# A sparse-attention and mixture-of-experts kernel: the first expert job's preparation cut into attention steps, later routing tables and weight conversion moved into the expert chunks

## The chip, the cores and the metric

The kernel runs on one core of a Trainium2 chip. The metric is the device time of one execution in microseconds. The median of 3 runs of the kernel before is 794.57 us (793.63 to 795.36).

## The reference

Three layers in float32. Attention over 4 batches, 8 heads, 576 positions and 64 columns per head; heads 0 to 3 see the last 32 positions (local mask), heads 4 to 7 every 32nd position (strided mask). Its output, as 2304 rows of 512, goes to a mixture of 8 experts, where each row is sent to the one expert with the highest logit:

```python
logits = x @ w_gate + modality_bias[modality_id]
e_idx = np.argmax(logits, axis=1)
gate_w = probs[np.arange(N), e_idx]                  # softmax of the logits
for e in range(E):                                   # E = 8
    mask = e_idx == e
    h = np.maximum(x[mask] @ w1[e], 0.0)             # w1: 512 x 1024
    out[mask] = gate_w[mask, None] * (h @ w2[e])     # w2: 1024 x 512
```

A dense layer follows: `h = x @ w_in` (512 x 2048), `g = where(h > 0, h, exp(min(h, 0)) - 1)`, `g @ w_out`.

## The kernel before

Three stages share one order of instructions written out by hand: each engine runs its instructions in the order in which the Python code emits them, and waits on semaphores where data come from another engine. So an instruction that waits holds up everything emitted behind it on its engine.

**Attention** is 32 steps n (one of 4 batches, one of 4 pairs of heads, one half). Steps with n mod 8 in 0 to 3 work on strided heads (tiles of 72 x 72), the others on local heads (96 x 128). Step n emits `emit_S(n)` (scores into both banks of "S", then on VectorE masks and row maxima, 8 or 6 fused instructions at L1009, then on GpSimd the subtraction of the maxima at L1010), transposes of the next queries and keys (`emit_T`, L976), `emit_PT(n-2)`, `emit_X(n-5)` and `emit_PV(n-3)`, and `emit_exp(n-1)` on ScalarE. Scores of step n+1 need the two "S" banks back from the masks of step n. Half of the tokens (tiles 0 to 8, `NE = 9`) have their logits after step 21.

**Background.** From step 21 on, a generator `early()` prepares the first expert job, job 0: it chooses the expert of each of the first 1152 tokens, picks a frequent expert, counts places, builds a one-hot table on GpSimd (L373), multiplies it with the token numbers on TensorE (`tab_ps`, L393), gathers 512 rows by indirect DMA (L448), splits the first weights (L468, L469), scales the rows by their gates (L452) and transposes them (`trans`, L463). `bg()` is called after single VectorE instructions of `emit_X` and `emit_PV` and emits the generator's work up to its next `yield`; a `yield STEP` holds it until the next step.

**Experts.** `NS = 5` jobs of 512 rows in 8 chunks each, 40 chunks g. `stream()` emits a chunk as 8 pieces, 4 of the first product and 4 of the second one of chunk g-2. The list `plan` puts other work between the pieces by their number: the rest of attention, `choose` for the second half of the tokens (10), `place` (14), the tables (`first_tables` 16, its product 28; `more_tables(20)` 30, product 36; `more_tables(36)` 36, product 44; `dense` 53, product 64), job 1's gathers (28), scaling (38) and transposes (42, 46, 52). `conv.unit()` converts a part of the dense layer's float64 weights; it runs after chunks g = 2 to 38 with (g-2) mod 5 in 0, 1, 3.

**Dense layer.** 80 steps, each with 12 products up and 6 or 12 down. The change touches nothing of it, but 12 of the conversion units lie there, as before.

SP's queue carries nearly all loads: queries, keys and values, the expert weights (`fetch`, two DMAs of 256 KB a chunk, two to four chunks ahead), the stores of `x_dram`, the raw and converted dense weights. GpSimd's queue carries the gathers.

Of the kernel before, what the change touches and what calls it, by code (L numbers as in the profile page):

```python
# [14 lines left out]
ALU = mybir.AluOpType  # L15
# [58 lines left out]
class Background:  # L74
# [20 lines left out]
    def step(self):  # L95
        self.held = False

    def finish(self):
# [70 lines left out]
class Router:  # L169
# [104 lines left out]

    def early(self, pool, chosen):

# [21 lines left out]
        V.scalar_tensor_tensor(pr, rank[:, 0:NE], -4096.0, z, ALU.add, ALU.mult)  # L298
        yield
        V.reduce_sum(pos, pr, axis=AX.X)  # L300
# [6 lines left out]
        chosen()  # L307
        yield from self.split_places(0, NE)
        onehot = self.new_onehot(pool)
        yield from self.onehot(0, NE, onehot, self.tc.nc.gpsimd)  # L310
        finish = self.table(pool, onehot, 0, NE, 0, 4, 5, self.idx, self.gates, self.tc.nc.gpsimd)
        yield Background.STEP
        V.tensor_scalar(no, pos, 512.0, None, ALU.is_ge)
        V.tensor_scalar(self.oh[:, 0:NE, 0], pos, 512.0, None, ALU.is_lt)
        yield
        V.tensor_tensor(oh, oh, no.unsqueeze(2).to_broadcast(sh), ALU.mult)
        yield
        finish()
        yield

    def place(self, pool):
# [82 lines left out]
def ffn(tc, ctx, x_dram, part_dram, ident, router, conv, bank, w1, w2, out, run_attention):  # L404
# [151 lines left out]
    def fetch_to(g):  # L556
        while loaded[0] <= g:
            s, f = divmod(loaded[0], NCH)
            if s < NS:
                if s == len(jobs):  # L560
                    new_job(s)
                raws[loaded[0]] = fetch(jobs[s], f)
            else:
                fetch2(loaded[0] - NG)
            loaded[0] += 1
# [26 lines left out]
    def early():  # L592
        STEP = Background.STEP
        yield from router.choose(0, NE)
        yield from router.early(r_p, lambda: fetch_to(2))
        for c in range(4):
            gather(jobs[0], c)
            yield STEP if c % 2 else None
        for i in range(SPLIT):
            split_to(i)  # L600
            fetch_to(i + AHEAD - SPLIT)
            yield STEP
        for c in range(4):
            scale(jobs[0], c)
            yield STEP if c == 3 else None
        for kk in range(4):
            trans(jobs[0], kk)
            yield STEP if kk % 2 else None

# [6 lines left out]
    def close_b():  # L616
        at.close_b()
        wp = ctx.enter_context(tc.tile_pool(name="w3", bufs=1))
        add_weights(wp, NW - len(WH))
        XT.extend(x_pairs(wp, 2))  # L620
        conv.start(ctx)

    def first_tables():
        oh[0] = router.new_onehot(r_p)
        run(router.onehot(0, NT, oh[0]))
        fin.append(router.table(r_p, oh[0], 0, NT, 4, 20, 5, idx, gate))
        router.blocks(r_p)

    def more_tables(c0):
        fin.append(router.table(r_p, oh[0], 0, NT, c0, c0 + 16, 5, idx, gate))  # L630

    def dense():
        oh[0] = router.new_onehot(r_p)
        run(router.onehot(1, NT, oh[0]))
        fin.append(router.table(r_p, oh[0], 1, NT, 0, NT, 2, idxd, None))

# [4 lines left out]
    def run(gen):  # L641
        for _ in gen:
            pass

    oh, fin = {}, []
    table = lambda: fin.pop()()

    def stream():

        for g in range(NG + LAG):  # L650
# [18 lines left out]
            if g >= LAG:  # L669
# [3 lines left out]
                yield from gemm2(jobs[s], f)  # L673
            if 2 <= g < NG - 1 and (g - 2) % 5 in (0, 1, 3):
                conv.unit()
# [10 lines left out]
        (5, lambda: at.L(3, 0)), (5, lambda: at.X(31)), (8, lambda: at.L(3, 1)),  # L686
        (10, lambda: at.lg(NE, NT)), (10, lambda: run(router.choose(NE, NT))), (10, close_b),
        (14, lambda: run(router.place(r_p))), (16, first_tables),
        (28, table), (28, lambda: new_job(1)), (30, lambda: more_tables(20)), (36, table), (36, lambda: more_tables(36)), (44, table),
        (53, dense), (64, table), (66, open_y),  # L690
    ]
    plan += [(28, lambda c=c: gather(jobs[1], c)) for c in range(4)]
    plan += [(38, lambda c=c: scale(jobs[1], c)) for c in range(4)]
# [20 lines left out]


    lctx = ExitStack()
    x_loop, h_loop = bank("T", "x_ps"), bank("S", "h_ps")
# [120 lines left out]
def attention(tc, bg, q, k, v, mod, mbias, wg, x_dram, ident, router, bank):  # L838
# [148 lines left out]
    def emit_S(n):  # L987
# [16 lines left out]
        mx = m_p.tile([m, 2 * nj], F32, tag="mx", name="mx")  # L1004
        for r in range(2):
            for j in range(nj):
                mk = mask_s if pr >= 2 else (mask_0 if s == 0 and j == 0 else mask_l)
                i = nj * r + j
                nc.vector.tensor_tensor_reduce(sm[:, i], pss[r][:, j], mk, 1.0, -3.0e38, ALU.add, ALU.max, mx[:, i:i + 1])  # L1009
        nc.gpsimd.tensor_tensor(sm, sm, mx.unsqueeze(2).to_broadcast([m, 2 * nj, w]), ALU.subtract)  # L1010
        st[n] = sm
# [111 lines left out]
    for n in range(NU):  # L1123
# [29 lines left out]
        if n > 8 and n % 8 == 3:  # L1153
            load_vl(n // 8)
    emit_exp(NU - 1)
    return SimpleNamespace(PT=emit_PT, PV=emit_PV, X=emit_X, L=emit_L, lg=emit_lg, close_a=actx.close, close_b=bctx.close)
# [28 lines left out]
```

## Time and profile before

| | |
|---|---|
| median of 3 runs | 794.57 us (793.63 to 795.36) |
| the profiled execution's own time | 794.71 us |
| its span, first to last instruction | 793.0 us |
| TensorE busy (matmuls) | 763.6 us, 96% of the span |
| VectorE / ScalarE / GpSimd busy | 508.3 / 395.6 / 108.5 us |
| mean granted TensorE clock | 0.991 |

The span and the profiled execution's own time differ by 1.7 us, which lie outside of the first and last instruction. TensorE is idle for 793.0 - 763.6 = 29.4 us. A granted clock of 1.00 is 2.4 GHz, one of 0.5 is 1.2 GHz; a value between them in a short stretch says that both levels occurred in it.

### The profile page before, as it was taken

What the parts mean: (1) busy time and instruction counts of PE and PEld (TensorE: products, weight loads), DVE (VectorE), ACT (ScalarE), POOL (GpSimd) and SP (SyncE); (2) the same over time, 40 slices, a digit from 0 to 9 for tenths busy, and PEclk for the clock granted to TensorE, in tenths of its full rate; (3) what the DMA queues carried; (4) which work ended last, traced back from release to release, by engine and by line L of the source; (5) the groups of instructions that cost most, each with busy time, mean ns of one, the idle gap of its engine ahead of it and who ended that gap; (6) DMA issues with size and microseconds to landing.
All of it is one profiled execution on the core that took longest, in us unless ns stands there. A gap on an engine that the chain in (4) does not pass through costs nothing.

```text
span 793.0 us, 12672 instructions
## 1 busy us (share of the span) xinstructions
PE 763.6 (96%) x4513; PEld 636.5 (80%) x4513; DVE 508.3 (64%) x1321; ACT 395.6 (50%) x759; POOL 108.5 (14%) x140
## 2 busy tenths in 40 slices
PE   6999988989999999999899999999999999999995
PEld 5989876868888888888788788888888888888885
DVE  3768779798867677576477565565666454544443
ACT  3667646433544454445376555554565444444442
POOL 4533372022001020000000101001001010101011
PEclk9999999999999999999999999999999999999999
DMA  9587695545566575454232221033133030201111
GB/s 159 120 186 172 151 241 102 153 148 186 179 204 222 172 227 183 163 184 136 93 122 80 94 79 54 27 107 119 41 95 131 1 107 0 84 24 41 66 41 67
DMA packets 100302, 94.37 MB, mean 119 GB/s; under 512 B 45433, under 2 KB 78731, under 8 KB 100235
## 3 DMA queue, kind: packets, MB, share of 16 engines
q1 hardware_dynamic: 95056, 78.79, 34.8%
q0 software_dynamic: 4480, 14.68, 5.4%
q8 instruction: 37, 0.61, 0.3%
q14 instruction: 30, 0.25, 0.1%
q10 hardware_dynamic: 699, 0.04, 0.1%
HBM read 70.95 MB, written 22.54 MB: 118 GB/s over the span
## 4 chain that ended last, share of the span: by engine, by line
PE 50%; POOLq 0%; POOL 0%; DVE 0%; issue 0%
PE o_ps L797 8%; PE o_ps L799 8%; PE o_ps L798 8%; PE h_ps L711 8%; PE h_ps L710 8%; PE h_ps L712 8%; POOLq L1181 0%; POOL out_dram L813 0%; DVE part L812 0%
## 5 line engine op out<-in xcount | busy, mean ns | idle before, releaser
L773 DVE SCALAR_TENSOR_TENSOR t<-e,t 128x512 f32<-128x512 f32 (+1 forms) x80 | 51.1, 638 | 110.7 <-ACT e L771 110.7
L710 PE MATMUL h_ps<-xh,wh 128*128 128x512 f32 (+1 forms) x320 | 119.1, 372 | 2.2 <-PEq L723 2.2
L712 PE MATMUL h_ps<-xh,wl 128*128 128x512 f32 (+1 forms) x320 | 119.3, 373 | 0.0
L711 PE MATMUL h_ps<-xl,wh 128*128 128x512 f32 (+1 forms) x320 | 119.2, 372 | 0.0
L797 PE MATMUL o_ps<-wh,gh 128*128 128x512 f32 x288 | 113.3, 393 | 0.0
L798 PE MATMUL o_ps<-wl,gh 128*128 128x512 f32 x288 | 112.9, 392 | 0.0
L799 PE MATMUL o_ps<-wh,gl 128*128 128x512 f32 x288 | 112.9, 392 | 0.0
L770 ACT ACTIVATE t<-h_ps 128x512 f32<-128x512 f32 (+1 forms) x80 | 44.2, 552 | 99.8 <-PE h_ps L712 92.3
L775 ACT CAST gh<-r 128x512 fp32r<-128x512 f32 (+1 forms) x80 | 46.2, 578 | 81.5 <-DVE r L774 81.5
L776 DVE TENSOR_TENSOR gl<-r,gh 128x512 fp32r<-128x512 f32 (+1 forms) x80 | 51.1, 639 | 51.5 <-ACT gh L775 51.5
L469 DVE TENSOR_TENSOR wl<-wraw,wh 128x1024 fp32r<-128x1024 f32 x56 | 69.2, 1235 | 12.8 <-ACT wh L468 11.0
L710 PEld LDWEIGHTS h_ps<-xh,wh 128*128 128x128 f32 x320 | 60.6, 189 | 14.3 <-issue 2.6
L711 PEld LDWEIGHTS h_ps<-xl,wh 128*128 128x128 f32 x320 | 60.6, 189 | 11.9
L712 PEld LDWEIGHTS h_ps<-xh,wl 128*128 128x128 f32 x320 | 60.5, 189 | 11.0
L504 PE MATMUL y_ps<-hh,wh 128*128 128x512 f32 x160 | 64.6, 404 | 0.0
L797 PEld LDWEIGHTS o_ps<-wh,gh 128*128 128x128 f32 x288 | 54.1, 188 | 12.5 <-DVE o L808 0.7
L799 PEld LDWEIGHTS o_ps<-wh,gl 128*128 128x128 f32 x288 | 54.1, 188 | 12.1
L485 PE MATMUL h_ps<-xh,wh 128*128 128x512 f32 x160 | 63.7, 398 | 0.0
L506 PE MATMUL y_ps<-hh,wl 128*128 128x512 f32 x160 | 63.3, 395 | 0.0
L505 PE MATMUL y_ps<-hl,wh 128*128 128x512 f32 x160 | 63.2, 395 | 0.0
L798 PEld LDWEIGHTS o_ps<-wl,gh 128*128 128x128 f32 x288 | 54.1, 188 | 11.1
L487 PE MATMUL h_ps<-xh,wl 128*128 128x512 f32 x160 | 62.9, 393 | 0.0
(180 smaller groups left out, 1393.4 us busy)
## 6 DMA issues: line engine op xcount, KB each, us to landing
wraw<-in_moe_w_dram SPq DMA_DIRECT2D x80, 256.0 KB
raw<-in_moe_w_in_dram SPq DMA_DIRECT2D x16, 512.0 KB
raw<-in_moe_w_out_dram SPq DMA_DIRECT2D x16, 512.0 KB
w_f<-cv_r SPq DMA_DIRECT2D x32, 256.0 KB
wraw<-w_f SPq DMA_DIRECT2D x16, 512.0 KB
part_dram<-o POOLq DMA_DIRECT2D x18, 256.0 KB, 3.0
part<-part_dram SPq DMA_DIRECT2D x18, 256.0 KB
qn<-in_q_dram SPq DMA_DIRECT2D x8, 288.0 KB
```

What stands on the lines that cost most here:

```text
L469: nc.vector.tensor_tensor(WL[i], raw, WH[i].bitcast(F32), ALU.subtract)
L485: nc.tensor.matmul(ps, lhsT=a, rhs=job.xh[kk], start=kk == 0, stop=False)
L487: nc.tensor.matmul(ps, lhsT=b, rhs=job.xh[kk], start=False, stop=kk == 3)
L504: nc.tensor.matmul(ps, lhsT=a, rhs=hh, start=f == 0, stop=False)
L505: nc.tensor.matmul(ps, lhsT=a, rhs=hl, start=False, stop=False)
L506: nc.tensor.matmul(ps, lhsT=b, rhs=hh, start=False, stop=f == NCH - 1)
L710: nc.tensor.matmul(ps[:, 0:n], lhsT=a, rhs=yh, start=kk == 0, stop=False)
L711: nc.tensor.matmul(ps[:, 0:n], lhsT=a, rhs=yl, start=False, stop=False)
L712: nc.tensor.matmul(ps[:, 0:n], lhsT=b, rhs=yh, start=False, stop=kk == 3)
L797: nc.tensor.matmul(ps, lhsT=a, rhs=WH[i][:, 512:1024], start=first, stop=False)
L798: nc.tensor.matmul(ps, lhsT=a, rhs=WL[i][:, 512:1024], start=False, stop=False)
L799: nc.tensor.matmul(ps, lhsT=b, rhs=WH[i][:, 512:1024], start=False, stop=last)
```

## The change

Four parts. (1) `bg.flush()` at the end of each attention step emits all background work up to the next `STEP`, in place of one piece after each VectorE instruction; the `STEP` marks are set anew, the weights are fetched chunk by chunk (`fetch_to(0)`, `(1)`, `(2)`, `(3)`) instead of three chunks at once, and job 0's rows are scaled on GpSimd instead of VectorE. The three instructions that take job 0's rows out of the counts become `others()` and move behind the second `choose` at piece 10. (2) In strided steps the 8 fused mask-and-maximum instructions become two additions over 288 columns and one maximum over 576. (3) The tables that no early job needs move: `more_tables(20)` from piece 30 to 84, `more_tables(36)` from 36 to 104, the dense table from 53 to seven parts at 120 to 144, their products to 100, 116 and 164. Their buffers come from a new pool. (4) Conversion units run from chunk 6 on, 7 in 10 chunks (24 units) in place of 3 in 5 from chunk 2 on (23 units).

```diff
--- before.py
+++ after.py
@@ -94,6 +94,11 @@
 
     def step(self):
         self.held = False
+
+    def flush(self):
+
+        while self.gens and not self.held:
+            self()
 
     def finish(self):
         while self.gens:
@@ -272,7 +277,7 @@
         V.tensor_copy(self.lof[:, q, 0:n], self.lo[:, q, 0:n])
         yield
 
-    def early(self, pool, chosen):
+    def early(self, pool, chosen, more):
 
         V = self.tc.nc.vector
         t = lambda shape, dt, name: pool.tile(shape, dt, name=name)
@@ -296,7 +301,7 @@
         yield
 
         V.scalar_tensor_tensor(pr, rank[:, 0:NE], -4096.0, z, ALU.add, ALU.mult)
-        yield
+        yield Background.STEP
         V.reduce_sum(pos, pr, axis=AX.X)
         V.tensor_tensor(key[0:1], key[0:1], self.rev[0:1], ALU.mult)
         yield
@@ -306,17 +311,23 @@
         V.tensor_scalar(self.star, kmax[0:1], -1.0, float(E), ALU.mult, ALU.add)
         chosen()
         yield from self.split_places(0, NE)
+        yield Background.STEP
         onehot = self.new_onehot(pool)
-        yield from self.onehot(0, NE, onehot, self.tc.nc.gpsimd)
+        for i, _ in enumerate(self.onehot(0, NE, onehot, self.tc.nc.gpsimd)):
+            yield Background.STEP if i == 1 else None
         finish = self.table(pool, onehot, 0, NE, 0, 4, 5, self.idx, self.gates, self.tc.nc.gpsimd)
+        more()
         yield Background.STEP
-        V.tensor_scalar(no, pos, 512.0, None, ALU.is_ge)
-        V.tensor_scalar(self.oh[:, 0:NE, 0], pos, 512.0, None, ALU.is_lt)
-        yield
-        V.tensor_tensor(oh, oh, no.unsqueeze(2).to_broadcast(sh), ALU.mult)
-        yield
         finish()
         yield
+
+        def others():
+
+            V.tensor_scalar(no, pos, 512.0, None, ALU.is_ge)
+            V.tensor_scalar(self.oh[:, 0:NE, 0], pos, 512.0, None, ALU.is_lt)
+            V.tensor_tensor(oh, oh, no.unsqueeze(2).to_broadcast(sh), ALU.mult)
+
+        self.others = others
 
     def place(self, pool):
 
@@ -592,20 +603,23 @@
     def early():
         STEP = Background.STEP
         yield from router.choose(0, NE)
-        yield from router.early(r_p, lambda: fetch_to(2))
+        yield STEP
+        yield from router.early(r_p, lambda: fetch_to(0), lambda: fetch_to(1))
         for c in range(4):
             gather(jobs[0], c)
-            yield STEP if c % 2 else None
-        for i in range(SPLIT):
-            split_to(i)
-            fetch_to(i + AHEAD - SPLIT)
-            yield STEP
+            yield STEP if c == 1 else None
+        split_to(0)
+        fetch_to(2)
+        yield STEP
+        split_to(1)
+        fetch_to(3)
+        yield
         for c in range(4):
-            scale(jobs[0], c)
-            yield STEP if c == 3 else None
+            scale(jobs[0], c, nc.gpsimd)
+            yield STEP if c == 1 else None
         for kk in range(4):
             trans(jobs[0], kk)
-            yield STEP if kk % 2 else None
+            yield STEP if kk % 2 == 0 else None
 
     bg.early = early
     at = run_attention(bg)
@@ -619,20 +633,24 @@
         add_weights(wp, NW - len(WH))
         XT.extend(x_pairs(wp, 2))
         conv.start(ctx)
+        late.append(tctx.enter_context(tc.tile_pool(name="late", bufs=1)))
 
     def first_tables():
-        oh[0] = router.new_onehot(r_p)
+        oh[0] = router.new_onehot(late[0])
         run(router.onehot(0, NT, oh[0]))
-        fin.append(router.table(r_p, oh[0], 0, NT, 4, 20, 5, idx, gate))
+        fin.append(router.table(late[0], oh[0], 0, NT, 4, 20, 5, idx, gate))
         router.blocks(r_p)
 
     def more_tables(c0):
-        fin.append(router.table(r_p, oh[0], 0, NT, c0, c0 + 16, 5, idx, gate))
-
-    def dense():
-        oh[0] = router.new_onehot(r_p)
-        run(router.onehot(1, NT, oh[0]))
-        fin.append(router.table(r_p, oh[0], 1, NT, 0, NT, 2, idxd, None))
+        fin.append(router.table(late[0], oh[0], 0, NT, c0, c0 + 16, 5, idx, gate))
+
+    def dense(i):
+        if i == 0:
+            oh[0] = router.new_onehot(late[0])
+            oh[1] = router.onehot(1, NT, oh[0])
+        next(oh[1], None)
+        if i == NT // 3:
+            fin.append(router.table(late[0], oh[0], 1, NT, 0, NT, 2, idxd, None))
 
     def open_y():
         rctx.close()
@@ -642,7 +660,8 @@
         for _ in gen:
             pass
 
-    oh, fin = {}, []
+    oh, fin, late = {}, [], []
+    tctx = ExitStack()
     table = lambda: fin.pop()()
 
     def stream():
@@ -671,7 +690,7 @@
                 if f == NCH - 1 and s:
                     jobs[s].start = start_of(router.tab[0:1, s, 1:2])
                 yield from gemm2(jobs[s], f)
-            if 2 <= g < NG - 1 and (g - 2) % 5 in (0, 1, 3):
+            if 6 <= g < NG - 1 and (g - 6) % 10 not in (3, 6, 9):
                 conv.unit()
             if g == NG - 1:
 
@@ -684,11 +703,12 @@
         (3, lambda: at.PV(30)), (3, lambda: at.X(29)), (3, lambda: at.PT(31)),
         (4, lambda: at.PV(31)), (4, lambda: at.X(30)),
         (5, lambda: at.L(3, 0)), (5, lambda: at.X(31)), (8, lambda: at.L(3, 1)),
-        (10, lambda: at.lg(NE, NT)), (10, lambda: run(router.choose(NE, NT))), (10, close_b),
+        (10, lambda: at.lg(NE, NT)), (10, lambda: run(router.choose(NE, NT))), (10, lambda: router.others()), (10, close_b),
         (14, lambda: run(router.place(r_p))), (16, first_tables),
-        (28, table), (28, lambda: new_job(1)), (30, lambda: more_tables(20)), (36, table), (36, lambda: more_tables(36)), (44, table),
-        (53, dense), (64, table), (66, open_y),
+        (28, table), (28, lambda: new_job(1)), (66, open_y),
+        (84, lambda: more_tables(20)), (100, table), (104, lambda: more_tables(36)), (116, table), (164, table),
     ]
+    plan += [(120 + 4 * i, lambda i=i: dense(i)) for i in range(NT // 3 + 1)]
     plan += [(28, lambda c=c: gather(jobs[1], c)) for c in range(4)]
     plan += [(38, lambda c=c: scale(jobs[1], c)) for c in range(4)]
     plan += [(n, lambda kk=kk: trans(jobs[1], kk)) for kk, n in enumerate((42, 46, 52, 52))]
@@ -713,6 +733,7 @@
 
 
 
+    tctx.close()
     lctx = ExitStack()
     x_loop, h_loop = bank("T", "x_ps"), bank("S", "h_ps")
     ahead = [bank("ST"[j], "h2_ps") for j in range(2)]
@@ -1003,10 +1024,15 @@
         sm = s_p.tile([m, 2 * nj, w], F32, tag="sm", name="sm")
         mx = m_p.tile([m, 2 * nj], F32, tag="mx", name="mx")
         for r in range(2):
+            if pr >= 2:
+                nc.vector.tensor_tensor(sm[:, nj * r:nj * r + nj], pss[r], mask_s.unsqueeze(1).to_broadcast([m, nj, w]), ALU.add)
+                continue
             for j in range(nj):
-                mk = mask_s if pr >= 2 else (mask_0 if s == 0 and j == 0 else mask_l)
+                mk = mask_0 if s == 0 and j == 0 else mask_l
                 i = nj * r + j
                 nc.vector.tensor_tensor_reduce(sm[:, i], pss[r][:, j], mk, 1.0, -3.0e38, ALU.add, ALU.max, mx[:, i:i + 1])
+        if pr >= 2:
+            nc.vector.reduce_max(mx, sm, axis=AX.X)
         nc.gpsimd.tensor_tensor(sm, sm, mx.unsqueeze(2).to_broadcast([m, 2 * nj, w]), ALU.subtract)
         st[n] = sm
 
@@ -1152,6 +1178,7 @@
             load_vs(n // 8 + 1)
         if n > 8 and n % 8 == 3:
             load_vl(n // 8)
+        bg.flush()
     emit_exp(NU - 1)
     return SimpleNamespace(PT=emit_PT, PV=emit_PV, X=emit_X, L=emit_L, lg=emit_lg, close_a=actx.close, close_b=bctx.close)
 
```

## Rows read from the trace of the kernel before

**Rows 1.** Waits of TensorE: in total us, times, longest us
```profile
PE ps_tr L976 <- DMA qn<-in_q_dram: 3.0, 3, 1.3
PE tab_ps L393 <- DVE A L388: 2.9, 1, 2.9
```
**Rows 2.** Stretches: us, busy us of each engine, clock, DMA share, GB/s
```profile
110.00:115.00 5.00, 4.33 (x41) 4.04 (x39) 4.04 (x28) 2.46 (x6) 4.31 (x4) 0.68 1.05 277
...
175.00:180.00 5.00, 5.00 (x23) 4.09 (x21) 4.35 (x9) 0.00 (x0) 2.01 (x3) 0.69 0.93 330
...
123.41:127.78 4.37, 3.31 (x40) 2.70 (x38) 4.14 (x14) 3.39 (x6) 1.45 (x1) 1.00 0.54 112
127.78:133.42 5.64, 4.89 (x42) 3.73 (x42) 5.61 (x25) 2.78 (x6) 1.47 (x1) 1.00 0.01 3
133.42:136.00 2.58, 1.00 (x8) 0.82 (x9) 2.51 (x10) 0.98 (x2) 1.47 (x1) 1.00 0.57 145
```
**Rows 3.** Timeline of TensorE: start, us, instruction, idle before
```profile
108.42 0.37 PE L393 MATMUL tab_ps<-A,onehot 128*128 128x20 bf16 x9 [1.91 <-POOL A L388]
...
115.65 0.44 PE L976 MATMUL ps_tr<-ident,qn 96*128 96x96 f32 x3 [1.32 <-DMA qn<-in_q_dram]
...
174.35 1.16 PE L393 MATMUL tab_ps<-A,onehot 128*128 128x80 bf16 x18 [2.90 <-DVE A L388]
...
180.81 0.72 PE L463 MATMUL x_ps<-ident,xg 128*128 128x128 f32 x4
```
**Rows 4.** Timeline of GpSimd
```profile
2.58 1.83 POOL L914 MEMSET vs<- 64x2080 f32 x1
...
99.54 1.15 POOL L1010 TENSOR_TENSOR sm<-sm,mx 72x576 f32<-72x576 f32 x1 [2.62 <-ACT sm L1014]
101.55 5.26 POOL L373 TENSOR_SCALAR onehot<-iota,pos_lof 128x128 bf16<-128x128 bf16 x9 [0.86 <-DVE rs L1061]
...
107.87 0.50 POOL L388 TENSOR_TENSOR A<-oa,vals 128x180 bf16<-128x180 bf16 x1
108.32 1.16 POOL L1010 TENSOR_TENSOR sm<-sm,mx 72x576 f32<-72x576 f32 x1
...
123.40 1.47 POOL L1010 TENSOR_TENSOR sm<-sm,mx 96x768 f32<-96x768 f32 x1 [5.64 <-DVE mx L1009]
...
171.52 1.57 POOL L448 DMA_INDIRECT xg<-x_dram,idx  x1 [14.89 <-DMA wraw<-in_moe_w_dram]
...
176.67 0.95 POOL L448 DMA_INDIRECT xg<-x_dram,idx  x1 [0.30 <-issue]
```
**Rows 5.** Timeline of VectorE
```profile
99.90 0.82 DVE L303 TENSOR_SCALAR pos<-pos 128x9 f32<-128x9 f32 x1
...
106.87 2.71 DVE L316 TENSOR_TENSOR oh<-oh,no 128x72 bf16<-128x72 bf16 x1
...
168.69 0.41 DVE L143 TENSOR_SCALAR cv_t<-raw 128x512 int32<-128x512 int32 x1
169.13 0.69 DVE L144 SCALAR_TENSOR_TENSOR cv_t<-raw,cv_t 128x512 int32<-128x512 int32 x1
...
170.60 0.17 DVE L396 SCALAR_TENSOR_TENSOR idx<-tab_sb 128x16 int32<-128x16 f32 x1
...
179.42 0.87 DVE L452 TENSOR_SCALAR xg<-xg,gates 128x512 f32<-128x512 f32 x2
```
**Rows 6.** Groups of instructions, 0 to 260 us, by shape: busy us, mean ns, idle
```profile
L1009 DVE CUSTOM_DVE_ANT_0 sm<-ps_sc,mask_s 72x72 f32<-72x72 f32 x128 | 20.6, 223 | 9.2 <-PE ps_sc L1001 9.2
...
L1066 DVE TENSOR_TENSOR xs<-ps_v,rs 72x256 f32<-72x256 f32 x32 | 12.1, 415 | 0.5
...
L340 DVE TENSOR_REDUCE pos<-places 128x36 f32<-128x324 f32 x1 | 0.5, 491 | 0.0
```
**Rows 7.** Queue of SP, timeline: the query loads of the last pair
```profile
109.12 1.42 SPq L875 DMA_DIRECT2D qn<-in_q_dram  x2
```
**Rows 8.** Tile xg (gathered rows), 100 to 260 us: issue to landing
```profile
DMA to landing us min/median/max: 4.0/5.2/7.6
```

## The prediction, made before the changed kernel ran

> **What bounds the kernel now.** I read the totals first: TensorE is busy for 96% of the span, so a change can gain only where TensorE is idle or slow. The list of its waits, then its timeline, say where. After 181 us it waits only at the check that leads to the dense layer, which isn't touched; all that this change can win lies in two places, steps 21 to 31 of attention and the first six expert chunks. There the reader is to see four things. TensorE waits 1.91 us for the table that GpSimd multiplies, 1.32 us for the queries of the last pair and 2.90 us for a table that VectorE multiplies [rows 1, 3]. After the 1.91 and after the 2.90 the granted clock of a 5 us stretch is 0.68 and 0.69, which is the 2.4 GHz level with the 1.2 GHz level in it, at 5 x 0.32 = 1.6 us of work lost; after the 1.32 it isn't [rows 2]. In steps 30 and 31 and up to the first expert product VectorE is busy 4.14 + 5.61 + 2.51 of 12.59 us and TensorE only 3.31 + 4.89 + 1.00 = 9.20 [rows 2], so VectorE sets the pace there and 3.4 us could be won. And in the experts the stall of 2.90 us has slack behind it: job 1's first transposes start at 180.81, just behind the scaling that began at 179.42 [rows 3, 5].
>
> **Steps 21 to 27.** `flush` puts each group of background work as a lump between the `emit_PV` of a step and the masks of the next one on VectorE. Until now pieces stood between other instructions and filled their latencies. VectorE is nearly always busy here, so what counts is what now stands ahead of the masks of step 24. New ahead of them are the nine small instructions that end in the places (L300 to L272), at about 0.13 us each, since one takes 0.17 us alone and the next starts earlier [rows 5]: 1.2 us (bounds: nothing if they fill gaps, 2.0 if one waits as L303 did for 0.82). So GpSimd's subtraction of step 24 starts not at 99.54 but at 100.74. Behind it GpSimd has 1.15 for it, nine one-hot rows of 5.26 in all, the subtraction of step 25 at 1.15 and the product A at 0.45 [rows 4]. The sum is 108.75. Splitting the nine into 6 and 3 changes their order, not their sum, and TensorE's table product still stands at the end of step 26, so it starts 0.4 later than at 108.42 [rows 3]. The stall stays and the slow stretch of 1.6 us behind it too. The masks in the new form cost VectorE more: 8 fused at 20.6/128 = 0.16 are 1.3 us a step; two additions at 0.41 (0.378 for 256 columns, times 288/256) and one maximum of 576 columns, between 0.49 (324 columns) and 0.87 (in proportion), say 0.75, are 1.6 [rows 6]. That is 0.3 a step, 4.5 us in 16 steps. I cost it at nothing on the path, since TensorE waits for the banks, which now come back after 0.8 instead of 1.3; if that cover is gone, steps 24 to 27 cost 1.2 more.
>
> **Step 28.** The last queries are issued at 109.12 behind three chunks of weights, 1.5 MB [rows 7]. Now one chunk stands ahead of them on SP's queue, and the second follows them. They come some 3 us earlier and the wait of 1.32 goes [rows 3]; step 29 starts 0.4 - 1.3 = 0.9 earlier. What is moved behind, values and two chunks, is needed from step 31 and from chunk 1 on.
>
> **Steps 29 to 31.** Here is the price. The rows are now scaled on GpSimd, two at the end of step 28 and two at the end of step 29, and the first transposes stand right behind them in TensorE's order, ahead of the scores of step 30. TensorE must wait for: the masks of step 29, GpSimd's subtraction behind them (at 123.40 before [rows 4]), and two scalings. GpSimd's price for a scaling of 128x512 isn't in the trace. The nearest rows are a fill at 1.83/2080 a column, 0.45 for 512, and a comparison of 128 columns at 5.26/9 = 0.58, 2.3 in proportion [rows 4]; I take 1.0, near the fill, since a fixed part is in the 0.58. Also, the second weight split on VectorE stands beside the first two scalings. The row shows what such neighbours do: L316, 72 columns, took 2.71 us, to 109.58, while GpSimd ran A and the subtraction to 109.48 [rows 4, 5]. I take 0.7 us for that (bounds 0 and 2.3). So the subtraction starts at 123.40 - 0.9 + 0.7 = 123.2, ends at 124.7, and the transposes start at 126.7. TensorE comes there at 123.41 - 0.9 = 122.5, where step 30 began before [rows 2], and idles for 4 us. From there its own work is the 9.20 of rows 2, to 135.9, and the clock falls, as after 1.91 and 2.90: 137.5, against 136.0. Attention ends 1.5 us later. With the bounds it is between 2 earlier (0.45, no neighbours, no slow stretch) and 6 later.
>
> The Trainium skill, page "SBUF — State Buffer", section "Who interferes with whom", names as those that contend with GpSimd the VectorE instructions in a two-port mode or with both inputs in SBUF, and says that the loser waits for the whole instruction. The trace agrees for L316. By that rule the weight split waits for both scalings, 1.3 us more than I took, and the sum would be 1.3 higher.
>
> **Experts up to chunk 6.** `others()` adds three VectorE instructions behind `choose`, and TensorE's `place` needs their result: 0.8 us (0.5 by three at 0.17, 3.2 if GpSimd is in the way as for L316 [rows 5]). It delays TensorE and VectorE alike. The conversion of chunk 3 no longer stands ahead of the first table's read-out: 0.41 + 0.69 = 1.1 less [rows 5]. So the row numbers of job 1, at 170.60 before, come at 170.3. The four gathers take from 171.52 to 176.67 to issue [rows 4]; without the neighbouring tables perhaps 4.0, so the last goes at 175.2. From issue to landing it takes 4.0 at least, 5.2 in the median [rows 8]; before it was about 4.0, since the last of the four scalings began by 180.7. I take 4.5, and 0.5 for the scaling: 180.2. TensorE, without the stall of 2.90 and the 1.6, is there at 180.81 - 2.90 - 1.6 + 0.8 = 177.1 and waits for 3 us. So the transposes start 0.6 earlier than at 180.81, but the slow stretch, which before lay in the shadow of this chain, now comes after it: -0.6 + 1.6 = +1.0 (bounds: -1.1 without it, +2.1 at the median landing). The tables and the conversions that come later lie under expert products, in a stretch where TensorE waits for nothing, and cost nothing; if that cover fails, one table costs what it did, 2.9.
>
> **The rivals.** A: the sum, 1.5 + 1.0 = 2.5 later. B: the waits only change their names, and no slow stretch is added: -0.1 and -0.6, so 794.0. For it speaks that 1.32 and 1.6 us of waiting left the clock alone; against it that the two waits I expect are 3 and 4. C, faster: scaling on GpSimd is done when TensorE gets there, because a scaling takes 0.45 to 0.7 and the split doesn't wait. Its place is the end of step 29; it decides if the transposes start before 124.3, a wait of under 1.9. Then attention ends at 133.4, 2.6 earlier, and with B's or A's experts it is 791.5 to 793.1. For it speaks VectorE's load in steps 30 and 31, which it lifts. D: GpSimd takes 2.3 a scaling: the transposes start at 131, and it ends near 801. E, that the change does not do what it says: the tables leave chunk 5 and nothing is won, since the gather sets that time anyway; it is part of A and B.
>
> The page "GPSIMD Engine Reference", section 4.1, of the Trainium skill holds that instructions with one input run on GpSimd at roughly line rate. The row of the fill bears it out, that of the comparison doesn't. By it a scaling would be about 0.65, an estimate from that page, and case C has its chance from there.
>
> **How the numbers follow.** The sum is made against the profiled execution: 794.7 + 2.5 = 797.2. It lies 0.14 above the median of the runs, so the forecast is 797.1. What a measurement here can tell from no change is about 0.2%, 1.6 us: below 793.0 is faster, above 796.2 slower. Chances: A 0.45 (795.0 to 799.5), B 0.22 (793 to 796), C 0.25 (789 to 793.3), D 0.08. Slower: most of A and all of D, 0.46; same: the rest of A and most of B, 0.27; faster: C and the edge of B, 0.27. The range of 8 in 10 takes in C and A and leaves out D: 790.0 to 800.0.
>
> **What would show it.** In the profile after: the wait of the small table on GpSimd near 108.8; no wait for queries in step 28; a wait of job 0's first transposes for scaled rows on GpSimd, near 4 us, with a slow stretch behind it; no wait for A at chunk 5, but one of about 3 us of job 1's transposes for gathered rows. The prediction is wrong if scaling on GpSimd takes under 0.7 us or over 2, if steps 23 to 26 lose more than 1 us to late masks, or if the gathers land sooner than 4 us after their issue.

## The result, and the profile after

The changed kernel takes 802.01 us in the median of 9 runs (797.06 to 805.55), the kernel before 795.06 us (793.63 to 798.60) beside it on the same chip: a ratio of 1.0082, with a 95% interval of 1.0058 to 1.0105. It is slower, by 7 us where the forecast said 2.5, and 802.0 lies outside the range that was given. The profiled execution spans 800.3 us, 7.3 more than before.

The waits of TensorE after, longest in total first (us in total, times, longest):

```profile
PE x_ps L474 <- DVE xg L463: 7.8, 4, 5.0
PE ps_tr L997 <- POOL vs L936: 4.6, 1, 4.6
PE x_ps L474 <- POOL xg L463: 3.9, 2, 2.7
PE tab_ps L404 <- POOL A L399: 2.6, 1, 2.6
PE h_ps L730 <- PEq L744: 1.8, 1, 1.8
PE x_ps L474 <- DVE tab_sb L406: 1.0, 1, 1.0
PE ps_tr L997 <- DMA qn<-in_q_dram: 0.8, 1, 0.8
```

Against [rows 1] the wait for the table of VectorE is gone, and the one query wait that is left (0.76 us, at 49.88) lies far ahead of step 21. New are the two kinds of `x_ps`: 3.9 us for job 0's rows, scaled on GpSimd, and 7.8 us for job 1's rows. The timeline of TensorE shows where they stand:

```profile
106.80 0.37 PE L404 MATMUL tab_ps<-A,onehot 128*128 128x20 bf16 x9 [2.58 <-POOL A L399]
...
123.55 0.33 PE L474 MATMUL x_ps<-ident,xg 128*128 128x128 f32 x1 [2.69 <-POOL xg L463]
125.09 0.48 PE L474 MATMUL x_ps<-ident,xg 128*128 128x128 f32 x1 [1.21 <-POOL xg L463]
...
175.93 0.30 PE L474 MATMUL x_ps<-ident,xg 128*128 128x128 f32 x1 [0.53 <-DVE xg L463]
176.79 0.33 PE L474 MATMUL x_ps<-ident,xg 128*128 128x128 f32 x1 [0.56 <-DVE xg L463]
182.11 0.47 PE L474 MATMUL x_ps<-ident,xg 128*128 128x128 f32 x1 [4.99 <-DVE xg L463]
184.31 0.47 PE L474 MATMUL x_ps<-ident,xg 128*128 128x128 f32 x1 [1.73 <-DVE xg L463]
```

Stretches behind these waits (busy us of TensorE's products, of its weight loads, of VectorE, ScalarE and GpSimd, then the granted clock, DMA share and GB/s; compare [rows 2]):

```profile
105.00:110.00 5.00, 3.20 (x42) 3.10 (x42) 3.08 (x9) 1.61 (x5) 4.38 (x7) 0.80 1.10 250
110.00:115.00 5.00, 5.00 (x55) 4.53 (x54) 3.62 (x16) 3.51 (x9) 4.53 (x4) 0.86 1.13 302
125.00:130.00 5.00, 4.91 (x36) 4.41 (x37) 2.56 (x14) 2.62 (x5) 1.28 (x2) 0.50 0.01 2
180.00:185.00 5.00, 1.16 (x3) 0.79 (x4) 0.97 (x2) 0.18 (x1) 0.00 (x0) 0.50 0.18 62
185.00:190.00 5.00, 5.00 (x14) 3.81 (x13) 2.44 (x3) 1.94 (x3) 0.00 (x0) 0.51 0.00 0
```

In the last one TensorE is busy throughout and gets 0.51, the 1.2 GHz level: after the wait of 7.8 us it works from 184.31 to about 189.9 at half clock, 2.8 us of work lost.

Where the time went, by the start of the same instruction on TensorE in both traces:

| up to | before | after | later in this part by |
|---|---|---|---|
| scores of step 4 | 23.21 | 21.31 | -1.90 |
| scores of step 27 | 108.72 | 107.10 | +0.28 |
| scores of step 29 | 119.10 | 116.13 | -1.35 |
| first expert product | 136.01 | 135.11 | +2.07 |
| product of the first large table | 164.98 | 164.81 | +0.73 |
| last transposes of job 1 | 189.51 | 194.43 | +5.09 |
| first product of the dense layer | 389.33 | 396.50 | +2.25 |

Of the first line 0.42 us come from the masks: from the scores of step 1 to those of step 2 it is 2.82 us in each of the five profiles with the old form and 2.40 in the twelve with the new one, since TensorE gets the banks back sooner there. The rest is the landing of the first loads, which the change doesn't touch; step 4 starts anywhere from 21.05 to 22.64 in the profiles with the new masks and from 21.45 to 23.21 in those with the old ones, so the early start belongs to these two executions and not to the change. What counts is the sixth line, and the other engines tell why. VectorE in front of job 1's transposes, GpSimd's gathers and SP's queue, after:

```profile
172.88 1.22 DVE L480 TENSOR_TENSOR wl<-wraw,wh 128x1024 fp32r<-128x1024 f32 x1 [0.24 <-ACT wh L479]
175.30 0.48 DVE L463 TENSOR_SCALAR xg<-xg,gates 128x512 f32<-128x512 f32 x1 [1.19 <-DMA xg<-x_dram,idx]
176.25 0.49 DVE L463 TENSOR_SCALAR xg<-xg,gates 128x512 f32<-128x512 f32 x1 [0.47 <-DMA xg<-x_dram,idx]
181.57 0.49 DVE L463 TENSOR_SCALAR xg<-xg,gates 128x512 f32<-128x512 f32 x1 [4.83 <-DMA xg<-x_dram,idx]
183.77 0.49 DVE L463 TENSOR_SCALAR xg<-xg,gates 128x512 f32<-128x512 f32 x1 [1.72 <-DMA xg<-x_dram,idx]
...
170.26 1.62 POOL L459 DMA_INDIRECT xg<-x_dram,idx  x1 [14.17 <-DVE gates L410]
...
175.23 0.95 POOL L459 DMA_INDIRECT xg<-x_dram,idx  x1 [0.30 <-issue]
...
171.00 0.38 SPq L486 DMA_DIRECT2D wraw<-in_moe_w_dram  x1
...
174.13 0.38 SPq L486 DMA_DIRECT2D wraw<-in_moe_w_dram  x1
174.71 0.35 SPq L488 DMA_DIRECT2D wraw<-in_moe_w_dram  x1
175.11 0.43 SPq L131 DMA_DIRECT2D raw<-in_moe_w_in_dram  x1
```

VectorE itself waits for the rows: the last gather is issued at 175.23 and its scaling starts at 183.77, 8.5 us later. Between 174.13 and 175.11 SP issued 1 MB, the weights of chunk 10 and the first conversion load. In the kernel before, the weights of chunk 10 were issued at 179.52, behind all gathers, because their buffer came free only when VectorE had split chunk 7 (the load starts 0.03 us behind the split's end, before and after). VectorE and SP of the kernel before:

```profile
176.70 1.66 DVE L388 TENSOR_TENSOR A<-oa,vals 128x1440 bf16<-128x1440 bf16 x1
178.28 1.21 DVE L469 TENSOR_TENSOR wl<-wraw,wh 128x1024 fp32r<-128x1024 f32 x1
...
179.52 0.38 SPq L475 DMA_DIRECT2D wraw<-in_moe_w_dram  x1
```

The split stood behind the tables that the change moved away. After, the same split begins at 172.88, 5.4 us sooner.

### The profile page after: what moved, and what is told of

It reads as the page before. It is cut to its first block, busy times and chain, and to the rows that moved or that the text cites. A ratio compares the mean times of both kernels' runs of the same rounds, so it can differ in the third digit from the quotient of the medians.

```text
span 800.3 us, 12473 instructions
## 1 busy us (share of the span) xinstructions
PE 766.7 (96%) x4513; PEld 638.1 (80%) x4513; DVE 507.7 (63%) x1109; ACT 395.8 (49%) x759; POOL 116.1 (15%) x144
## 5 line engine op out<-in xcount | busy, mean ns | idle before, releaser
L497 PE MATMUL h_ps<-xl,wh 128*128 128x512 f32 x160 | 63.2, 395 | 0.0
```

Of the source, the lines that this page charges most:

```text
L497: nc.tensor.matmul(ps, lhsT=a, rhs=job.xl[kk], start=False, stop=False)
```

## The experiments

Times are medians; each ratio is against runs of the kernel before on the same chip, with its 95% interval. Not all runs were made on one chip, so where two runs are compared with each other their ratios count; 0.0010 is 0.8 us. Four runs undo or hold back something in the changed kernel and one repeats it, four do one part in the kernel before and one adds the held loads to such a part, five look for a better version.

**VectorE scales job 0's rows again.**

```diff
-            scale(jobs[0], c, nc.gpsimd)
+            scale(jobs[0], c)
```

> The changed kernel, with the four rows of job 0 scaled on VectorE as before. Theory (GpSimd's 1.6 us a scaling stands in TensorE's order): the waits of job 0's first transposes, 2.7 + 1.2 us, go, and with them about half of the slow stretch behind them, while VectorE gets 4 x 0.49 us more; attention ends some 3 us earlier and the whole comes to 799 us. Rival (VectorE sets the pace in steps 29 to 31, whoever scales): the 2 us on VectorE and a later second weight split take it back, 802 us, no difference.

Measured: 797.94 us, ratio 1.0022 (1.0003 to 1.0042), 4 to 5 us better than the changed kernel, where the theory had 3. But not all of it is job 0's: a wait of 2.05 us stays there, now for VectorE's scaling, since the transposes still stand right behind it; and in this profile the last row block of job 1 came 6.7 us after its issue (174.59 to 181.28), not 8.5.

**The tables back at their old places, the rest of the change kept.**

```diff
-        (84, lambda: more_tables(20)), (100, table), (104, lambda: more_tables(36)), (116, table), (164, table),
+        (30, lambda: more_tables(20)), (36, table), (36, lambda: more_tables(36)), (44, table), (64, table),
     ]
-    plan += [(120 + 4 * i, lambda i=i: dense(i)) for i in range(NT // 3 + 1)]
+    plan += [(53, lambda i=i: dense(i)) for i in range(NT // 3 + 1)]
```

> The changed kernel, with the two later routing tables and the dense one back at their old places in chunks 4 to 8. Theory (the tables' work on VectorE held the weight split of chunk 7, this held the load of chunk 10, and so the gathered rows of job 1 came in 4.3 us): the wait for a table at chunk 5 is back, 2.9 us, but the rows land in 4 to 5 us again instead of 8.5, and the transposes of job 1 follow the scaling; 802 - 5 = 797 us. Rival (the gathers are late for another reason): 2.9 us and the slow stretch come on top, 803 to 806 us.

Measured: 794.99 us, ratio 0.9978 (0.9956 to 1.0000). The whole loss of 7 us hangs on the tables' places. A wait for a table is back (1.8 us), the weights of chunk 10 are issued at 179.82, and the last row, issued at 177.31, is scaled at 181.96, 4.7 us later.

**The two loads held until job 1's rows are scaled.** A small transfer on SP's queue reads the scaled rows, so SP issues what follows only then. It writes one column of a scratch buffer that is written over later. The changed kernel with this one line more:

```diff
+    plan += [(38, lambda: nc.sync.dma_start(part_dram[NT - 1, :, 0:1], jobs[1].xg[3][:, 0:1]))]
```

> The changed kernel with one small transfer more on SP's queue: it reads one column of the last scaled row block of job 1, so that the weights of chunk 10 and the first conversion load are issued only when job 1's rows have been gathered and scaled. Theory (these two loads, 1 MB, delay the gathers): the last gather lands 4 to 5 us after its issue, the transposes wait some 4 us instead of 7.8 and the slow stretch is shorter; 802 - 5 = 797 us. Rival (the gathers take 6 to 8 us whatever stands beside them): the wait stays 7 to 8 us and the time 802; held loads come late for chunk 10 and it may be slower still.

Measured: 797.09 us, ratio 1.0024 (1.0004 to 1.0044). VectorE, GpSimd and SP of this kernel:

```profile
179.41 0.49 DVE L463 TENSOR_SCALAR xg<-xg,gates 128x512 f32<-128x512 f32 x1 [0.74 <-DMA xg<-x_dram,idx]
180.71 0.49 DVE L463 TENSOR_SCALAR xg<-xg,gates 128x512 f32<-128x512 f32 x1 [0.81 <-DMA xg<-x_dram,idx]
...
175.03 1.49 POOL L459 DMA_INDIRECT xg<-x_dram,idx  x1 [0.30 <-issue]
176.82 0.94 POOL L459 DMA_INDIRECT xg<-x_dram,idx  x1 [0.30 <-issue]
...
181.22 0.33 SPq L714 DMA_DIRECT2D part_dram<-xg  x1
181.82 0.39 SPq L486 DMA_DIRECT2D wraw<-in_moe_w_dram  x1
```

The last row comes 3.9 us after its issue, not 8.5, and the transposes wait 3.3 us, not 7.8. By the ratios 4.6 us come back. The theory stands, and the rival falls.

**The conversion from chunk 8 on, so that of the two loads only the weights stand beside the gathers.**

```diff
-            if 6 <= g < NG - 1 and (g - 6) % 10 not in (3, 6, 9):
+            if 8 <= g < NG - 1 and (g - 8) % 10 not in (4, 9):
```

> The changed kernel with the conversion units from chunk 8 on instead of 6, in a slightly denser pattern, so that their first load comes behind the gathers of job 1 and only the weights of chunk 10 stand beside them. If the conversion's load is what delays the rows, they land in 4 to 5 us and the time is 797 us, as with both loads held; if the weights are, 802 us as in the changed kernel; if each does its half, 799 to 800 us.

Measured: 798.90 us, ratio 1.0037 (1.0013 to 1.0062). The last row, issued at 176.81, is scaled at 182.24, 5.4 us later. So each load takes its part: with neither of them 3.9, with the weights alone 5.4, with both 6.7 to 8.5 us. The conversion's load alone was not run; its part is the difference.

**The changed kernel a second time.**

> The changed kernel once more, for a second profile. If the landing of job 1's rows is the same each time, the last gather lands 8 to 9 us after its issue again and the wait ahead of job 1's transposes is 7 to 8 us; if it scatters with the order of the packets, the two differ by 1 us or more (in the kernel with VectorE's scaling, which is the same in the experts, the last one took 6.7 us). The slow stretch after the wait of step 26 lasts 1.7 us of lost work, as in the first profile, or 4 to 5, as in two of the others.

Measured: 802.82 us. The last row, issued at 176.29, is scaled at 184.78: 8.5 us again, and the transposes wait 7.8 us again; against the 6.7 of the kernel with VectorE's scaling, which is the same in the experts, the landing scatters by some 2 us. So does the slow stretch behind the wait of step 26. First this profile, then that of the kernel with VectorE's scaling, whose instructions are the same up to there; the wait ahead is 2.59 us in both:

```profile
105.00:110.00 5.00, 2.65 (x35) 2.49 (x35) 3.31 (x12) 1.12 (x3) 4.63 (x7) 0.79 0.99 245
110.00:115.00 5.00, 5.00 (x41) 4.60 (x40) 2.71 (x8) 3.06 (x6) 4.05 (x4) 0.53 1.08 292
115.00:120.00 5.00, 5.00 (x64) 4.41 (x63) 3.88 (x20) 3.87 (x10) 3.00 (x2) 1.00 1.21 219
```

```profile
105.00:110.00 5.00, 2.79 (x42) 2.53 (x42) 3.34 (x11) 1.76 (x5) 4.49 (x6) 0.90 0.92 235
110.00:115.00 5.00, 5.00 (x41) 4.61 (x40) 3.38 (x13) 2.63 (x5) 4.42 (x4) 0.50 1.07 290
115.00:120.00 5.00, 5.00 (x38) 4.27 (x38) 1.64 (x13) 3.23 (x7) 1.91 (x2) 0.58 1.21 210
```

With the first profile (0.80 from 105 to 110 and 0.86 from 110 to 115, 1.7 us lost) that makes 1.7, 3.4 and 5.1 us of work lost for the same wait. Each of the three comes twice in the six profiles whose instructions are the same up to there: 1.7 also with the tables at their old places, 3.4 with the conversion from chunk 8, 5.1 with the held loads.

**Single parts in the kernel before**: the masks, the conversion from chunk 6, job 0's new preparation (with `flush` and `others`), and the tables' new places, each alone and as in the diff of the change.

> The kernel before with the mask edit alone (two additions and one maximum instead of eight fused instructions in the steps of the strided pairs). Theory (VectorE has the 0.3 us a step to spare, and step 4 starting 1.9 us earlier in the changed kernel's trace is an early load, not the masks, which do not come before step 4): 795 us, no difference. Rivals: TensorE gets the score banks back sooner and the 1.9 us are real, 793; or VectorE's 0.3 us a step lie on the path in steps 21 to 31, 796 to 797.

Measured: 794.56 us, ratio 0.9991 (0.9969 to 1.0013): no difference that the runs show; the 0.42 us of step 2 lie within the interval. (That the masks do not come before step 4 was an error: steps 0 to 3 are strided ones.)

> The kernel before with the conversion units from chunk 6 on alone. Theory (its work lies under expert products): 795 to 796 us, no difference. Rival (by itself it frees VectorE ahead of the stall for a table at chunk 5 and the 1.1 us are seen): 793 to 794.5 us.

Measured: 794.72 us, ratio 1.0002 (0.9983 to 1.0020): no difference.

> The kernel before with the new preparation of job 0 alone (the lumps, one chunk of weights ahead of the queries, scaling on GpSimd, the three instructions put off until behind the attention); masks, tables and conversion stay. Theory (two waits of 2.7 and 1.2 us for GpSimd's scaling against the query wait and VectorE's load in steps 30 and 31, which go): within 1 us of before, 795 us. Rival, the term of the forecast (attention ends 1.5 us later): 796.5 us.

Measured: 796.23 us, ratio 1.0011 (0.9990 to 1.0033). The interval holds both answers. The waits for GpSimd's scaling are there, 2.7 and 1.2 us.

> The kernel before with the later routing tables and the dense one moved as in the changed kernel, and nothing else. Theory (without the tables the weight split of chunk 7 ends early, the load of chunk 10 starts some 5 us sooner, and the gathers land late behind it): the wait of 2.9 us at chunk 5 is replaced by one of 4 to 8 us before the transposes of job 1, with a slow stretch behind it: 798 to 801 us. Rival (the tables' move is harmless by itself, the loss comes from the two preparations together): 793 to 795 us.

Measured: 801.54 us, ratio 1.0070 (1.0046 to 1.0095). This part alone makes the kernel slower by nearly as much as all four. The wait at chunk 5 is gone; its place in the list is taken by this:

```profile
PE x_ps L463 <- DVE xg L452: 6.1, 4, 3.3
```

**The tables' new places and the held loads, in the kernel before**, with the same small transfer.

> The kernel before with the tables moved (801.5 us alone) and the loads of chunk 10 and of the conversion at chunk 5 held until job 1's rows are scaled, by the same small transfer. Theory (those loads delay the gathers): rows land 3.5 to 4.5 us after their issue, 801.5 - 4 = 797 to 798 us. Rival (the rows are as late as that by the time of their issue alone): 800 to 802 us.

Measured: 797.58 us, ratio 1.0035 (1.0014 to 1.0056), 4.0 us less than with the tables alone by the medians, 2.8 by the ratios. The last row comes in 3.7 us (173.81 to 177.52) where it took 5.75 (173.85 to 179.60).

**A version to beat both.** On top of the held loads (`MID` is a new mark that holds the background work until before the next `emit_X`; its few lines are left out here):

```diff
...
-            scale(jobs[0], c, nc.gpsimd)
-            yield STEP if c == 1 else None
+            scale(jobs[0], c)
+            yield STEP if c == 1 else Background.MID if c == 3 else None
...
-        (84, lambda: more_tables(20)), (100, table), (104, lambda: more_tables(36)), (116, table), (164, table),
+        (84, lambda: more_tables(20)), (96, table), (96, lambda: more_tables(36)), (112, table), (164, table),
...
-    plan += [(n, lambda kk=kk: trans(jobs[1], kk)) for kk, n in enumerate((42, 46, 52, 52))]
+    plan += [(n, lambda kk=kk: trans(jobs[1], kk)) for kk, n in enumerate((48, 50, 52, 54))]
...
```

> A version to beat both: the changed kernel with the scaling of job 0 on VectorE and its first transposes in the middle of step 30, the loads of chunk 10 and of the conversion held until job 1's rows are scaled, job 1's transposes 2 to 6 pieces later in the stream (at 48, 50, 52 and 54), and the two later tables' products away from the transposes of job 2. Theory (each wait was met because TensorE came too early to rows that were on their way): no wait over 1 us between step 28 and chunk 8, 802 - 4 - 5 - 2 = 790 to 792 us. Rival (the work that stands at those places is only pushed and something else, such as the weights of chunk 10, comes late): 795 us and over.

Measured: 786.74 us, ratio 0.9882 (0.9854 to 0.9911): 1.2% faster than the kernel before and better than expected. TensorE's longest waits, and two of its stretches:

```profile
PE ps_tr L1003 <- DMA qn<-in_q_dram: 6.1, 4, 4.8
PE tab_ps L409 <- POOL A L404: 2.5, 1, 2.5
PE h_ps L736 <- PEq L750: 1.9, 1, 1.9
PE ps_tr L1003 <- DMA kn<-in_k_dram: 0.8, 1, 0.8
PE x_ps L479 <- DVE xl L473: 0.7, 1, 0.7
```

```profile
125.00:130.00 5.00, 4.33 (x54) 3.79 (x53) 4.93 (x24) 3.42 (x7) 1.47 (x1) 1.00 0.08 22
180.00:185.00 5.00, 5.00 (x26) 4.07 (x25) 4.09 (x6) 2.94 (x5) 3.08 (x3) 1.00 0.92 314
```

No wait for rows is left, of either job, and the clock stays at 1.00 where it was 0.50.

> The first combination (786.7 us) without the held loads. Theory (the loads delay the rows by some 3 to 4 us, of which the 4 us that the transposes were put off hide most): the first transposes of job 1 wait 1 to 4 us again, 788 to 791 us. Rival (putting the transposes off was all that was needed): 787 us.

Measured: 790.13 us, ratio 0.9932 (0.9911 to 0.9952). The transposes wait 2.6 us again; the last row, issued at 172.92, is scaled at 179.83, 6.9 us later. The theory's numbers; the hold is worth 3.4 us by the medians, 4.0 by the ratios, even where the transposes come later.

**The wait for the small table.** Three tries moved its product (and the gathers behind it) from the end of step 26.

```diff
...
         more()
-        yield Background.STEP
+        yield Background.MID
         finish()
-        yield
...
             gather(jobs[0], c)
-            yield STEP if c == 1 else None
+            yield
```

> The version before it, and the product of the first small table in the middle of step 27 instead of at the end of step 26, with the four gathers right behind it. Theory: the wait of 2.6 us for GpSimd goes and the slow stretch behind it with it, 2 to 5 us less than the version before it, 786 to 789 us. Rival (the rows of job 0 come later by as much and the transposes of step 30 or GpSimd's subtraction of step 28 wait for it): no difference to the version before it.

Measured: 792.21 us, ratio 0.9955 (0.9934 to 0.9976), 5.5 us worse than the first combination. It doesn't answer the question that it was made for: the product ended up ahead of `emit_PV` of step 26, 1.2 us earlier, not later. The wait grew from 2.5 to 3.8 us, and 110 to 120 us ran at 0.50; but 2.6 us were followed by about 10 us at half clock in two other profiles, so this run doesn't show that the longer wait made the stretch longer.

Then the product where it was meant to be (against the run above):

```diff
...
         more()
+        yield Background.STEP
         yield Background.MID
         finish()
```

> The first combination (786.7 us), with the product of the small table really later: at the X of step 27, some 2 us of TensorE's work behind its present place (the second combination had put it in the middle of step 26, 1.2 us earlier instead of later, and its wait was 3.8 instead of 2.5 us and TensorE at half clock for 10 us). Theory: the wait is under 0.5 us, no slow stretch follows, 786.7 - 2.5 - 1.7 = 782 to 784 us. Rival (GpSimd's four gathers then stand ahead of its subtraction of step 28, and something after it waits): 786 us or more.

Measured: 791.41 us, ratio 0.9940 (0.9919 to 0.9961). The wait is gone (0.28 us), but what it had covered now stands in the open: the weights of chunk 1, for which ScalarE waits 3.5 us with queries behind them, so that TensorE waits 3.0 us for ScalarE; and the gathered rows, for which VectorE waits 2.8 and 1.4 us with the masks behind them, so that TensorE waits 2.5 us for masks there.

And with the second split and the scaling a step later:

```diff
...
         fetch_to(2)
         yield STEP
+        yield STEP
         split_to(1)
```

> The combination with the table's product at the X of step 27, and the second weight split and the scaling of job 0 one step later than there, so that they do not wait for loads that are still on their way. Theory (in that version TensorE was 4 us earlier in step 28 than the weights of chunk 1 and the gathered rows): no wait of more than 1 us in steps 27 to 29, 783 to 786 us. Rival (the rows and VectorE's splits are then late for the first expert product): 787 us or more, no better than the first combination.

Measured: 786.31 us, ratio 0.9873 (0.9841 to 0.9906), level with the first combination. The second split no longer waits, but the scaling does (1.54 and 1.27 us, for the gathers), and TensorE waits 2.1 us for the masks behind it. So the rival holds: no better, with a new wait in the place of the old.

## Why the prediction was wrong, step by step

**The step that failed** is the landing of job 1's rows: "I take 4.5". From the row numbers to the last scaled row block the forecast has 9.9 us (170.3 to 180.2); it took 14.9 (169.35 to 184.26). Of the 5.0 us more, 4.0 are the landing, 8.5 instead of 4.5, and 1.0 is the issue of the four gathers, which took 5.0 us instead of 4.0 even without the tables beside it. The rows from which the 4.5 was taken held for a queue on which the next load came behind job 1's gathers, and the bounds stopped at the median, 5.2, although [rows 8] ends at 7.6. The prediction asked what a faster VectorE does to TensorE, not which buffer its weight split sets free and what SP issues then; the load of chunk 10 isn't in the diff at all. With the loads held the landing is back at 3.9 us in the changed kernel and at 3.7 in the kernel before with the tables moved, and 4.6 and 2.8 us of the time come back by the ratios (4.9 and 4.0 by the medians): this cause is shown. None of the prediction's signs of being wrong caught it, since it named only a landing of under 4 us.

**Mis-sized beside it.** The slow stretch behind this wait cost 2.8 us, not 1.6. The tables that later "cost nothing" cost 0.66 us of TensorE's time for each of two products (228.60 to 229.26 for the first), which in the kernel before stood where TensorE waits for job 1 or next to it; and behind one of them a transpose of job 2 waits 1.0 us until VectorE has read the product out (the line `tab_sb` in the list of waits). Together 2.3, the +2.25 of the table's last line.

The account, then: forecast 2.5; the attention 1.0 later instead of 1.5, -0.5; from there to job 1's last transposes 5.8 later instead of 1.0, +4.8; behind them +2.25; the early start -1.9. Together 7.2, near the 7.3 between the two spans. That the trace agrees so well with the 7 us of the medians is in part luck, since the early start isn't the change's. Within the 4.8 the parts (5.0 for the chain, 1.2 for the clock) make 1.4 more: 0.66 of this is the product that no longer stands between the transposes, 0.34 that three of the first four transposes were done during the wait (0.13 us are left behind it, not 0.47), and the other 0.4 is not accounted for.

**Right.** The small table: TensorE waits on (2.58 us), and its product was to come 0.4 later; the scores behind it come 0.28 later. The query wait goes, 1.3 us (-1.35). The masks cost nothing on the path; two additions and a maximum take 0.81 to 0.82 and 0.75 us, as estimated. Job 0's transposes wait about 4 us for GpSimd (3.9), and half clock follows. From step 29 to the first expert product the forecast's terms make +2.4 us; it is +2.07. The three instructions behind `choose` were to cost 0.8; that part is 0.73 longer. The row numbers of job 1 were to come 0.3 sooner, by the attention's end; they come at 169.35 where the attention ended 0.9 sooner, so 0.35 sooner by it.

**Right with a wrong size inside.** A scaling on GpSimd was taken at 1.0 us:

```profile
117.11 3.37 POOL L463 TENSOR_SCALAR xg<-xg,gates 128x512 f32<-128x512 f32 x2
...
121.94 3.10 POOL L463 TENSOR_SCALAR xg<-xg,gates 128x512 f32<-128x512 f32 x2
...
117.33 1.72 DVE L480 TENSOR_TENSOR wl<-wraw,wh 128x1024 fp32r<-128x1024 f32 x1
```

It takes 1.55 to 1.7 us. The comparison in [rows 4] in proportion (2.3) was as near as the fill (0.45), and between them lies the value. The first two transposes could go at 120.36, ahead of the second pair of scalings, GpSimd's subtraction ended at 121.96, 0.8 sooner than forecast even without the early start, and two scalings took 1.1 longer: that the wait came out alike is luck. The weight split beside the first pair took 1.72 us where the split ahead of it, at 113.02, took 1.21, 0.5 more against the 0.7 in the sum, and ended 1.4 ahead of the pair; it did not wait for both scalings, so the 1.3 us more that the prediction set beside its sum did not come. By the Trainium skill, page "GPSIMD Engine Reference", section 4.1 "Engine selection", an instruction with one input runs roughly at line rate. The 0.65 us that the prediction estimated from that is 2.4 times too low here, and case C, which had its chance from it, falls.

**Slips in the sums.** 0.378 us times 288/256 is 0.43, not 0.41, which leaves the 1.6 us a step as it is. At the median landing of 5.2 the experts' part comes to +1.7, not +2.1. And C asked for transposes before 124.3, while the sum's own rows give 124.9 at the least (the subtraction from 122.5, two scalings at 0.45).

**The rivals.** B and C were built on the same landing of 4.5; B fell with the two slow stretches (0.50 and 0.51 granted), C with the scalings. D gave the right time (near 801) by the wrong mechanism, a slow GpSimd. The mechanism that decided was not among them, although its rule can be found: the Trainium skill, page "DMA: Bandwidth & Descriptors", section "Queues, rings and completion order", says that each DMA engine takes turns between the queues that have work for it, a packet at a time. The landings of 3.9, 5.4 and 6.7 to 8.5 us with none, one and two loads issued on SP's queue ahead of the last gather agree with sharing of that kind; how the packets alternate no run here shows.

**Open.** How far single runs scatter, and why: 797.06 to 805.55 for the changed kernel. The landing (6.7 to 8.5 us) and the slow stretch of step 26 (1.7, 3.4 and 5.1 us of work lost in six profiles of the same instructions) could each move the time by some 2 to 3.5 us, but the runs at the ends were not profiled. Job 0's preparation alone is settled to no better than -0.8 to +2.6 us.

## What to carry to other kernels

When work is taken off an engine, follow not only who waits for it but what it sets free: a buffer that comes back sooner starts a transfer sooner, and one that was held back by chance may have left the path clear for a transfer that matters. A wait that covered others is worth little until those are moved too: put the consumer later, keep loads that aren't urgent behind the urgent gather, and a loss of 0.8% becomes a gain of 1.2% with nearly the same parts. Before an instruction is given to GpSimd, look for a row of its own kind; a fill is no guide to a scaling.

## What was not expected of the hardware

A gather of 128 rows of 2 KB is there 3.4 to 3.9 us after its issue when the last load on SP's queue was issued some 4 us ahead of it (six profiles), 5.4 with 0.5 MB more issued within 1.1 us ahead (one), and 6.7 to 8.5 with 1 MB issued within the same 1.1 us (four). With 1 MB issued 1.8 to 3.4 us ahead it took 5.75 (one, the tables alone). And where the gather's own issue took 2.2 to 2.3 us instead of 0.95, it was there 4.6 to 4.9 us after its start (four). A wait of the same length at the same place of the same instructions, 2.6 us in step 26, was followed by half clock for 3.4 us in two profiles, 6.8 in two and about 10 in two, with TensorE busy throughout behind it in all six. And GpSimd takes 1.55 us for a scaling of 128x512 that VectorE does in 0.49.
